# First loads in one queue, the third scaling behind the first maxima, the fourth weight a step later, and the memory term's transposes ahead of the products with V

## The chip, the cores and the metric

The kernel runs on one core of a Trainium2 chip. The time is in microseconds of the device, for one execution. The engines are TensorE (PE: matrix products and transposes; PEld: its weight loads), VectorE (DVE), ScalarE (ACT), GpSimd (POOL) and SyncE (SP), which here issues DMAs; ScalarE issues a few as well.

## What is computed

A block of three parts, over 4 x 8 heads, 576 positions and 64 values for each head:

```python
scores = scale * np.matmul(q, k.transpose(0, 1, 3, 2))
scores = np.where(causal, -1000000000.0, scores)
a = np.exp(scores - scores.max(-1, keepdims=True))
a /= a.sum(-1, keepdims=True) + 1e-09
local = np.matmul(a, v)
q_p = phi(q)                       # where(q > 0, q, exp(q) - 1) + 1
mem_out = (q_p @ M_prev) / (q_p . z_prev + 1e-06)
x = g * mem_out + (1 - g) * local  # g = sigmoid(beta), one for each head
x = ((x @ w1) * (x @ w2) @ w3) @ w_out
h = x @ w_in
out = (h - np.tanh(h)) @ w_out2
```

The weights come as 64-bit floats; the kernel decodes each tile of 128 x 512 of them into two 32-bit parts.

## The kernel before

The program has three stages. The first is attention (about 0 to 240 us), the second the two products `x @ w1` and `x @ w2` with the product that follows, the third `h` and the output. `w3` and `w_out` are multiplied with each other ahead of time, during attention ("folds"), which is why weights are decoded there.

Attention goes over 16 pairs of heads, each in four steps of query rows (`GROUPS`): blocks 0 and 1 of 128 rows, block 2, block 3, and the last 64 rows. A step `m` is numbered through, 64 in all, and the loop of lines 771 to 820 does two at once. In order of the text, one round does: `recip` and `norm` of the steps m-2 and m-1 (the reciprocal sums on VectorE, then the normalisation of the weights p on GpSimd); `scores` and `rmax` of m and m+1 (products into PSUM, maxima on VectorE); `work(m)`, which is the exponentials of step m on ScalarE and one round of the background list; the products with V, `av`, of the pair before; `flush_t`, the four transposes of one tile of the memory term (`mt<-ident,mw` in the rows), where one is due; some fold products (`pieces`, `fo` in the rows); the transposes `trans` of the normalised weights (`t<-ident,p`), each copied out of PSUM by ScalarE or VectorE; then `work(m + 1)`, more pieces and the transposes of the step after. Each engine runs its instructions in the order of this text (`Ordered`), so an instruction that waits holds up all behind it on its engine. `psT`, which takes the transposes of both kinds, has two PSUM tiles, and the scores have two as well (`SB`).

The background list (`background`, `decode`) decodes one weight tile at a time in several moves, one for each step: a clamp (`T<-raw`) and a scaling (`E<-raw`) on GpSimd, a scaling and a conversion on ScalarE, a joining on VectorE, which frees the raw buffer (there are three) for the next load, a rounding to the high part on GpSimd (`wa<-T`, `zs<-T` and the like) and the low part on VectorE. `m >= coming[0]` and `LEAD` set when the next tile begins: one step after the last for the first `LEAD` tiles, two steps after it from then on. Up to step `SHORT` = 9 the list comes behind the exponentials of a step, afterwards ahead of them.

The start: pair 0's q and k come in three pieces of 128, 192 and 256 columns (`qk_cols`, lines 334, 336 and 339), the first two in SP's queue, the third in ACT's, where the gates' `beta` stands behind it. VectorE scales q piece by piece (`first_q`, lines 350 to 352). `scores(0)` needs the first two pieces, `scores(1)` the third. `fill` puts products of a constant tile, which nothing reads, into TensorE's order: seven at the start, six ahead of step 2's scores and three ahead of its transposes.

Of the kernel before, what the change touches and what calls it, by code (L numbers as in the profile page):

```python
# [33 lines left out]
def block_kernel(ctx, tc, qk, qt, vt, mp, zp_d, beta, w1, w2, w3t, wo, wi, wo2, ident_d, mask_d, out):  # L34
# [26 lines left out]
    PE, DV, AC, PO, SP = [Ordered(e) for e in (nc.tensor, nc.vector, nc.scalar, nc.gpsimd, nc.sync)]  # L61
# [62 lines left out]
    class Decoder:  # L124
# [14 lines left out]
        def step(self):  # L139
            while self.loaded and len(self.active) < self.width:  # L140
                raw, dst = self.loaded.popleft()
                self.reading += 1
                self.active.append(dec_ops(raw, dst, self.lo_on, self.whole, self.hip, self.x))
            if not self.active:
                return False
            gen = self.active.popleft()
            r = next(gen, 2)
            if r == 1:
                self.reading -= 1
                self.load()  # L150
            if r == 2:
                self.done += 1
            else:
                self.active.append(gen)
            return True
# [14 lines left out]
    def mm(o, lhsT, rhs, start, stop):  # L170
        return PE.matmul(o, lhsT, rhs, start=start, stop=stop).ins
# [8 lines left out]
    ZB, FLAG, WAIT = 3, 1, 2  # L180
    PIECES = (1, 2, 0, 2)
    MEM, ROOM = 12, (1.5, 1.5, 1.75)
    LEAD, SHORT, TB, WX = 3, 9, 4, (0, 1, 2, 3, 4, 5)
    MS, FS, FS5 = 4, 3, 6
    FILL = {None: 7, "s": {2: 6}, "t": {2: 3}}
    PO_ = "xzw"
# [17 lines left out]
    def qk_cols(P, c, queue=SP):  # L204
        if P not in qk_t:
            qk_t[P] = apr.tile([128, 2, 576], F32, tag="r", name="r")
        queue.dma_start(out=qk_t[P][:, :, c], in_=qk[P].rearrange("p (a n) -> p a n", a=2)[:, :, c])

    def load_v(P):
        SP.dma_start(out=V[P % 2], in_=vt[P].rearrange("p (t h d) -> p t h d", t=5, h=2))  # L210
# [121 lines left out]
    if True:  # L332
# [3 lines left out]
        qk_cols(0, slice(128, 320))  # L336
        mraw = stg["T"].tile([128, 512], F32, tag="T", name="mraw")
        AC.dma_start(out=mraw[:, 0:128], in_=mask_d)
        qk_cols(0, slice(320, 576), AC)
        AC.dma_start(out=gates, in_=beta.partition_broadcast(128))  # L340
        warm = mraw[:, 128:512].bitcast(BF16)
        DV.memset(warm, 0)
# [3 lines left out]
        def first_q(a, e, P=0):  # L346
            q = qk_t[P][:, 0, a:e]
            DV.tensor_scalar(out=q, in0=q, scalar1=0.125, scalar2=None, op0=ALU.mult)

        first_q(0, 128)  # L350
        first_q(128, 320)
        first_q(320, 576)
        AC.activation(out=identb, in_=ident, func=AF.Copy)
        AC.activation(out=maskb, in_=mraw[:, 0:128], func=AF.Copy)
        AC.activation(out=gates, in_=gates, func=AF.Exp, scale=-1.0)
# [44 lines left out]
        def scores(m):  # L400
            P, us = step(m)
            q, k = qk_t[P][:, 0], qk_t[P][:, 1]
            hr = [(h, slice(64 * h, 64 * h + 64)) for h in range(2)]
            sc = sc_t[m] = pss.tile([128, 2, 512], F32, tag="sc", name="sc")
            qs = [(h, r, y, slice(64 * y, 64 * y + 64)) for y in range(2) for h, r in hr]
            for u, a in us:
                if u == 4:
                    continue
                K = 128 * (u + 1)
                for h, r, y, c in qs:  # L410
                    mm(sc[c, h, a:a + K], q[r, 128 * u + 64 * y:128 * u + 64 * y + 64], k[r, 0:K], True, False)
                for h, r, y, c in qs:
                    mm(sc[c, h, a + 128 * u + 64 * y:a + 128 * u + 128], identb[r, r], maskb[r, 0:128 - 64 * y], False, True)
            if us[0][0] == 4:
                for x in range(2):
                    for h, r in hr:
                        y = x ^ h
                        mm(sc[r, y, 0:288], q[r, 512:576], k[r, 288 * y:288 * y + 288], True, y == 0)
                for h, r in hr:
                    mm(sc[r, 1, 224:288], identb[r, r], maskb[r, 0:64], False, True)  # L420
# [185 lines left out]
        def mem_b(tl, qp):  # L606
            t = ps["t"]()
            for hp in range(4):
                tp(t[:, hp * 128:hp * 128 + 128], qp[:, hp * 128:hp * 128 + 128])
            for i in range(2):  # L610
                copy(mem_t["q"][i][:, :, tl * 128:tl * 128 + 128],
                     t[:, 256 * i:256 * i + 256].rearrange("p (a b) -> p a b", a=2),
                     on_act=i == 0 or not in_order[0])
# [72 lines left out]
        def flush(k, ok):  # L686
            if not (late and late[0][0] <= fstep[0] and late[0][1] == k and ok):
                return False
            _, _, x, y = late[0]
            return k == "t" or finished[0] >= 8 * ((x * N + N - 1) // 576) + 8  # L690

        def flush_t():
            if flush("t", True):
                _, _, x, y = late.popleft()
                mem_b(x, y)
                held[0] -= 1
# [14 lines left out]
        def background(m):  # L711
            used = [0, 0, 0]

            def advance(j):
                nonlocal used
                used = [u + n for u, n in zip(used, j[0])]
                j[0] = next(j[1], None)
                if j[0] is None:
                    jobs.remove(j)
                    active[0] -= j[2]  # L720

            for j in [*jobs]:
                if j[1] is not mem_job:
                    advance(j)
            if m >= coming[0] and begun[0] < len(fold_seq) and active[0] < TB:
                k = fold_seq[begun[0]]
                if k[0] not in range(8) or len(coming) - 1 - folded[0] < ZB + 2:
                    if k[0] in range(8):
                        coming.append(k)
                    begun[0] += 1  # L730
                    g = decode(raws[live[0]])
                    live[0] += 1
                    jobs.append([next(g), g, 1])
                    used[2] += 0.7
                    active[0] += 1
                    coming[0] = m + (1 if m < LEAD else 2)
            for j in [*jobs]:
                if j[1] is mem_job and not any(n and u + n > c for u, n, c in zip(used, j[0], ROOM)):
                    advance(j)
# [8 lines left out]
        def fill(n):  # L748
            for _ in range(n):
                mm(spare, warm[:, 0:128], warm[:, 128:640], True, True)  # L750
# [10 lines left out]
        def work(h):  # L761
            fstep[0] = h
            if h >= SHORT:
                background(h)
            if h < NM:
                exps(h)
            if h < SHORT:
                background(h)

        m = 0  # L770
        while m < NM + 3 or jobs or late or folded[0] < 16 or begun[0] < len(fold_seq):
            P, s = divmod(m, 4)
            fstep[0] = m
            if 2 <= m <= NM:
                for h in (m - 2, m - 1):
                    recip(h)
                for h in (m - 2, m - 1):
                    norm(h)
            if m < NM:
                fill(FILL["s"].get(m, 0))  # L780
                for h in (m, m + 1):
                    scores(h)
                    rmax(h)
                if m == 0:
                    set_gates()
                if m == 2:
                    first_q(0, 576, 1)
            work(m)
            if 1 <= P <= 16:
                av(P - 1, s // 2)  # L790
                if s == 2 and P + 1 < 16:
                    load_v(P + 1)
            trs = 0 <= m - WAIT < NM
            flush_t()
            pieces(m, PIECES[s])
            if trs:
                fill(FILL["t"].get(m, 0))
                for u in GROUPS[(m - WAIT) % 4]:
                    trans((m - WAIT) // 4, u)
            work(m + 1)  # L800
            sums = flush("o", True)
            if not (sums and not fold_open[0]):
                pieces(m + 1, PIECES[s + 1])
            if trs:
                for u in GROUPS[(m + 1 - WAIT) % 4]:
                    trans((m + 1 - WAIT) // 4, u)
            if sums and not fold_open[0]:
                flush_o()
            if s == 0 and 1 <= P <= 16 - RB:
                load_qk(P + RB - 1)  # L810
            if s == 0 and 1 <= P < 15:
                scale_q(P + 1)
            if not todo and not raws and not wdec[0]:
                wdec[0] = Decoder(w_items[NE:], 2, 3)
                wdec[0].done, wdec[0].total = NE, 16
            if m == NM - 2:
                gate.update({e.engine: tail[e.engine] for e in (AC, DV)})
            if m == NM:
                gate[PO.engine] = tail[PO.engine]
            m += 2  # L820
# [369 lines left out]
```

## Time and profile before

| | us |
|---|---|
| median of 3 runs | 968.78 (968.11 to 969.84) |
| the profiled execution | 971.45 |
| its span, first to last instruction | 969.7 |
| TensorE busy | 943.9 |
| VectorE, ScalarE, GpSimd busy | 675.8, 623.1, 408.1 |

A busy time is the sum of the engine's instructions. A row of the timeline gives the start, the time and, in brackets, how long the engine had been idle before it and whose work or transfer ended last. The granted clock is the share of TensorE's full clock in a stretch.

### The profile page before, as it was taken

To read this page: it belongs to the slowest core of one execution; us is meant where nothing else is said; L and a number is where in the kernel's file an instruction comes from. 1 tells how busy PE (TensorE), PEld (TensorE's weight loads), DVE (VectorE), ACT (ScalarE), POOL (GpSimd) and SP (SyncE) were. 2 spreads that over 40 slices of the span, in tenths; PEclk is the share of its full clock that TensorE was granted. 3 is DMA by queue.
4 is the path that set the end of the run, shared out by engine and by line. 5 is a ranking of instruction groups with operands and counts; after the bars stand their busy time and mean duration, and the time that the engine had idled before them with its cause. 6 is when DMAs were issued, how large, how long until landed. Compare 5 with 4: busy or idle time off the path is not lost.

```text
span 969.7 us, 16290 instructions
## 1 busy us (share of the span) xinstructions
PE 943.9 (97%) x5928; PEld 816.4 (84%) x5928; DVE 675.8 (70%) x1185; ACT 623.1 (64%) x1398; POOL 408.1 (42%) x500
## 2 busy tenths in 40 slices
PE   6899999999999999999999999999999999999998
PEld 3466666567989999999999999999999989999996
DVE  5778868897776743534424588887787887878875
ACT  5688887786546551323625587687777766776864
POOL 3768867786474521202406862222222222222222
PEclk9899999999999999999999999999999999999999
DMA  6455435422344530101401100000000000000000
GB/s 216 155 169 168 158 127 183 135 75 85 128 149 146 183 114 31 55 22 44 153 22 45 44 1 1 1 33 1 1 33 1 33 1 1 33 1 1 33 1 33
DMA packets 26080, 68.29 MB, mean 70 GB/s; under 512 B 4880, under 2 KB 5904, under 8 KB 26000
## 3 DMA queue, kind: packets, MB, share of 16 engines
q1 hardware_dynamic: 25296, 66.86, 20.8%
q8 instruction: 46, 0.75, 0.3%
q10 hardware_dynamic: 704, 0.40, 0.2%
q14 instruction: 34, 0.28, 0.1%
HBM read 62.53 MB, written 4.72 MB: 69 GB/s over the span
## 4 chain that ended last, share of the span: by engine, by line
PE 84%; DVE 7%; ACT 4%; POOL 2%; issue 1%; DMA 1%; ACTq 0%; DVEq 0%; POOLq 0%; SPq 0%
PE o L50 24%; PE h L50 21%; PE ab L50 19%; PE x L50 10%; PE sc L50 3%; PE t L50 3%; PE fo L50 3%; DVE st L50 2%; ACT p L50 2%; PE mo L50 2%; POOL p L50 1%; DMA r<-in_qk 1%; DVE g L50 1%; DVE mst L50 1%; DVE T L50 1%
## 5 line engine op out<-in xcount | busy, mean ns | idle before, releaser
L50 POOL TENSOR_TENSOR gl<-s,gh 128x384 fp32r<-128x384 f32 x96 | 99.7, 1038 | 288.0 <-ACT gh L50 274.9
L50 PE MATMUL x<-abh,wf 128*128 128x384 f32 x384 | 107.0, 342 | 1.1 <-ACT abh L50 1.1
L50 ACT ACTIVATE s<-u,pc 128x384 f32<-128x384 f32 x192 | 107.7, 613 | 0.6 <-POOL gl L50 0.6
L50 PE MATMUL ab<-xh,wa 128*128 128x384 f32 x384 | 106.9, 338 | 0.7 <-ACT xh L50 0.6
L50 POOL TENSOR_SCALAR p<-p,st 128x128 f32<-128x128 f32 (+2 forms) x144 | 86.1, 616 | 47.2 <-DVE st L50 41.0
L50 PE MATMUL ab<-xh,wb 128*128 128x384 f32 x384 | 105.9, 336 | 0.0
L50 DVE SCALAR_TENSOR_TENSOR s<-s,u 128x384 f32<-128x384 f32 x96 | 83.9, 874 | 26.8 <-ACT s L50 25.9
L50 ACT ACTIVATE p<-sc,st 128x128 f32<-128x128 f32 (+2 forms) x144 | 78.3, 556 | 29.7 <-DVE st L50 25.8
L50 ACT ACTIVATE u<-u,pc 128x384 f32<-128x384 f32 x96 | 59.4, 619 | 46.8 <-DVE s L50 46.8
L50 DVE TENSOR_TENSOR a<-ab,a 128x384 f32<-128x384 f32 x48 | 26.4, 552 | 77.4 <-PE ab L50 77.4
L50 PEld LDWEIGHTS x<-abh,wf 128*128 128x128 f32 x384 | 70.2, 188 | 5.6 <-issue 3.9
L50 POOL TENSOR_SCALAR E<-raw 128x512 f32<-128x512 f32 x72 | 53.9, 749 | 48.5 <-DVE z2p L50 13.1
L50 DVE TENSOR_TENSOR t<-h,t 128x384 f32<-128x384 f32 x96 | 53.1, 553 | 28.0 <-ACT t L50 27.5
L50 PEld LDWEIGHTS ab<-xh,wa 128*128 128x128 f32 x384 | 70.1, 188 | 2.0 <-ACT xh L50 0.9
L50 ACT ACTIVATE u<-h 128x384 f32<-128x384 f32 x96 | 46.7, 487 | 38.9 <-PE h L50 38.8
L50 PEld LDWEIGHTS ab<-xh,wb 128*128 128x128 f32 x384 | 70.1, 188 | 0.3 <-issue 0.3
L50 POOL TENSOR_SCALAR T<-raw 128x512 f32<-128x512 f32 x72 | 53.7, 746 | 39.2 <-DMA raw<-in_wo 12.0
L50 PE MATMUL sc<-r 64*64 64x128 f32 (+4 forms) x640 | 64.5, 457 | 5.8 <-DMA r<-in_qk 2.9
L50 DVE SCALAR_TENSOR_TENSOR s<-s,s 128x384 f32<-128x384 f32 x96 | 63.9, 665 | 8.7 <-DVE s L50 0.5
L50 PE MATMUL t<-ident,p 128*128 128x128 f32 (+1 forms) x400 | 58.2, 279 | 11.9 <-POOL p L50 4.4
L50 PEld LDWEIGHTS t<-ident,p 128*128 128x128 f32 (+1 forms) x400 | 45.2, 140 | 24.4 <-POOL p L50 6.4
L50 ACT ACTIVATE E<-raw 128x512 uint16<-128x512 uint32 x72 | 57.2, 795 | 12.6 <-POOL E L50 12.3
(208 smaller groups left out, 2538.3 us busy)
## 6 DMA issues: line engine op xcount, KB each, us to landing
raw<-in_wo SPq DMA_DIRECT2D x24, 512.0 KB, 3.5
r<-in_qk SPq DMA_DIRECT2D x15, 576.0 KB, 5.9
raw<-in_w3t SPq DMA_DIRECT2D x16, 512.0 KB, 4.0
raw<-in_w SPq DMA_DIRECT2D x16, 512.0 KB, 3.7
raw<-in_wi SPq DMA_DIRECT2D x16, 512.0 KB, 3.5
v<-in_vt SPq DMA_DIRECT2D x16, 320.0 KB, 2.9
mw<-in_qt SPq DMA_DIRECT2D x18, 256.0 KB, 3.5
out<-ob SPq DMA_DIRECT2D x18, 256.0 KB, 2.2
```

Of the source, the lines that this page charges most:

```text
L50: i = call(*args, **kw)
```

## The change

Four places. The third piece of pair 0 is loaded by SP's queue, behind the first two. Its scaling on VectorE stands behind the maxima of step 0. `LEAD` is 2 in place of 3, so that the fourth weight tile begins at step 4 in place of 3, and all after it later by one step (the last eight by two: the last at step 58, before at 56). `flush_t` stands ahead of `av`.

```diff
-    LEAD, SHORT, TB, WX = 3, 9, 4, (0, 1, 2, 3, 4, 5)
+    LEAD, SHORT, TB, WX = 2, 9, 4, (0, 1, 2, 3, 4, 5)
...
-        qk_cols(0, slice(320, 576), AC)
+        qk_cols(0, slice(320, 576))
         AC.dma_start(out=gates, in_=beta.partition_broadcast(128))
...
         first_q(0, 128)
         first_q(128, 320)
-        first_q(320, 576)
...
                 for h in (m, m + 1):
+                    if h == 1:
+                        first_q(320, 576)
                     scores(h)
                     rmax(h)
...
             work(m)
+            flush_t()
             if 1 <= P <= 16:
                 av(P - 1, s // 2)
                 if s == 2 and P + 1 < 16:
                     load_v(P + 1)
             trs = 0 <= m - WAIT < NM
-            flush_t()
             pieces(m, PIECES[s])
```

VectorE's first instructions (`r` holds q and k, `st` the maxima), before and then now:

```order
L50 TENSOR_SCALAR r<-r 128x128
L50 TENSOR_SCALAR r<-r 128x192
L50 TENSOR_SCALAR r<-r 128x256
L50 TENSOR_REDUCE st<-sc 128x2 x3
L50 TENSOR_SCALAR gates<-gates 128x16
```

```order
L50 TENSOR_SCALAR r<-r 128x128
L50 TENSOR_SCALAR r<-r 128x192
L50 TENSOR_REDUCE st<-sc 128x2 x2
L50 TENSOR_SCALAR r<-r 128x256
L50 TENSOR_REDUCE st<-sc 128x2
L50 TENSOR_SCALAR gates<-gates 128x16
```

The scaling of 256 columns has gone behind the two maxima of step 0 and stands ahead of the one of step 1.

GpSimd from the normalisation of steps 0 and 1 (`p` of 128 to 384 columns) to that of steps 2 and 3 (512 and 576 columns) and the next, before and then now:

```order
L50 TENSOR_SCALAR wa_275<-T 128x512
L50 TENSOR_SCALAR E<-raw 128x512
L50 TENSOR_SCALAR T<-raw 128x512
L50 TENSOR_SCALAR p<-p,st 128x512 x2
L50 TENSOR_SCALAR p<-p,st 128x576
L50 TENSOR_SCALAR wb_343<-T 128x512
L50 TENSOR_SCALAR E<-raw 128x512
L50 TENSOR_SCALAR wa_375<-T 128x512
L50 TENSOR_SCALAR T<-raw 128x512
L50 TENSOR_SCALAR p<-p,st 128x128 x2
```

```order
L50 TENSOR_SCALAR wa_275<-T 128x512
L50 TENSOR_SCALAR E<-raw 128x512
L50 TENSOR_SCALAR p<-p,st 128x512 x2
L50 TENSOR_SCALAR p<-p,st 128x576
L50 TENSOR_SCALAR wb_341<-T 128x512
L50 TENSOR_SCALAR T<-raw 128x512
L50 TENSOR_SCALAR wa_372<-T 128x512
L50 TENSOR_SCALAR E<-raw 128x512
L50 TENSOR_SCALAR p<-p,st 128x128 x2
```

The fourth weight's `T<-raw` has gone behind the normalisation; ahead of the one after it stand a rounding and an `E<-raw`, where a `T<-raw` stood.

TensorE around the third tile of the memory term (`o` is the product with V, `fo` a fold), before and then now:

```order
L50 MATMUL o<-g_2177,v_107 64x256 x2
L50 MATMUL o<-g_2177,v_107 64x128 x2
L50 MATMUL mt<-ident,mw 128x128 x4
L50 MATMUL fo<-fo_980,zs 128x512 x3
L50 MATMUL t<-ident,p 128x128 x8
L50 MATMUL fo<-fo_1177,zs 128x512 x3
L50 MATMUL fo<-fo_1374,zs 128x512 x3
L50 MATMUL t<-ident,p 128x128 x4
```

```order
L50 MATMUL mt<-ident,mw 128x128 x4
L50 MATMUL o<-g_2164,v_107 64x256 x2
L50 MATMUL o<-g_2164,v_107 64x128 x2
L50 MATMUL fo<-fo_1396,zs 128x512 x3
L50 MATMUL t<-ident,p 128x128 x12
```

The memory term's four transposes have gone ahead of the products with V, and two of the three groups of folds have left this round.

## Rows read from the trace of the kernel before

**Rows 1.** The page: busy time of each engine, over the whole span.

```profile
PE 943.9 (97%) x5928; PEld 816.4 (84%) x5928; DVE 675.8 (70%) x1185; ACT 623.1 (64%) x1398; POOL 408.1 (42%) x500
```

**Rows 2.** Windows: stretch, us, busy of the five engines, granted clock, DMA share, GB/s.

```profile
20.00:30.00 10.00, 6.11 (x63) 3.57 (x67) 7.29 (x17) 8.72 (x24) 6.74 (x10) 0.87 0.64 219
30.00:40.00 10.00, 9.66 (x94) 5.19 (x88) 7.06 (x17) 4.97 (x13) 6.28 (x12) 0.79 0.31 96
```

**Rows 3.** Timeline of TensorE from 6 to 31 us.

```profile
6.67 1.13 PE L50 MATMUL sc<-r 64*64 64x256 f32 x8 [1.40 <-DVE r L50]
...
10.76 1.87 PE L50 MATMUL sc<-r 64*64 64x384 f32 x8 [2.86 <-DMA r<-in_qk]
...
12.62 1.96 PE L50 MATMUL spare<-mraw 128*128 128x512 bf16 x6
14.51 1.09 PE L50 MATMUL sc<-r 64*64 64x512 f32 x8
...
25.40 0.33 PE L50 MATMUL t<-ident,p 128*128 128x128 f32 x1 [2.67 <-POOL p L50]
...
27.93 1.30 PE L50 MATMUL t<-ident,p 128*128 128x128 f32 x5 [0.88 <-DVE g L50]
29.16 1.99 PE L50 MATMUL sc<-r 64*64 64x512 f32 x8
```

**Rows 4.** Timeline of the other engines and SP's queue, 0 to 16 us.

```profile
0.73 1.32 SPq L50 DMA_DIRECT2D r<-in_qk  x2
...
10.74 0.29 DVE L50 TENSOR_SCALAR r<-r 128x256 f32<-128x256 f32 x1 [4.12 <-DMA r<-in_qk]
...
10.95 1.02 DVE L50 TENSOR_REDUCE st<-sc 128x2 f32<-128x256 f32 x2
...
11.62 0.64 POOL L50 TENSOR_SCALAR T<-raw 128x512 f32<-128x512 f32 x1
12.05 0.22 ACT L50 ACTIVATE gates<-gates 128x16 f32<-128x16 f32 x1 [7.15 <-DMA gates<-in_beta]
...
15.22 2.75 POOL L50 TENSOR_SCALAR p<-p,st 128x128 f32<-128x128 f32 x6 [2.97 <-DVE st L50]
```

**Rows 5.** DMA issues of 0 to 40 us: size, median us to landing.

```profile
r<-in_qk ACTq DMA_DIRECT2D x1, 256.0 KB, 9.1
r<-in_qk SPq DMA_DIRECT2D x1, 192.0 KB, 4.9
...
gates<-in_beta ACTq DMA_DIRECT2D x1, 8.0 KB, 9.7
```

**Rows 6.** Timeline of SP, GpSimd and ScalarE, 19 to 27 us.

```profile
19.10 0.33 SPq L50 DMA_DIRECT2D raw<-in_wo  x1
...
20.87 0.68 POOL L50 TENSOR_SCALAR E<-raw 128x512 f32<-128x512 f32 x1
...
23.07 0.64 POOL L50 TENSOR_SCALAR T<-raw 128x512 f32<-128x512 f32 x1 [1.52 <-DMA raw<-in_wo]
...
23.80 2.94 POOL L50 TENSOR_SCALAR p<-p,st 128x512 f32<-128x512 f32 x3
...
26.65 0.60 ACT L50 ACTIVATE g<-t 128x512 f32<-128x512 f32 x1 [0.94 <-PE t L50]
```

**Rows 7.** Timeline of TensorE: transposes after each memory tile, and one fold group.

```profile
89.56 0.63 PE L50 MATMUL t<-ident,p 128*128 128x128 f32 x4 [0.62 <-ACT g L50]
...
90.72 0.85 PE L50 MATMUL fo<-wb,zs 128*128 128x512 f32 x3
...
123.83 0.66 PE L50 MATMUL t<-ident,p 128*128 128x128 f32 x4 [1.04 <-DVE mq L50]
...
166.31 0.66 PE L50 MATMUL t<-ident,p 128*128 128x128 f32 x4 [1.27 <-ACT g L50]
```

**Rows 8.** Waits, whole span: us in total, times, longest.

```profile
POOL p L50 <- DVE st L50: 41.0, 23, 3.4
...
PE t L50 <- POOL p L50: 4.4, 5, 2.7
```

## The prediction

> **What bounds the kernel now.** I read the page's busy line first, then the windows and the granted clock, then TensorE's own order of time, then the engines that its early waits name. TensorE is busy for 943.9 of 969.7 us [rows 1], so only 25.8 us of idle time and whatever runs at the lower clock can be won; work moved on another engine counts only where TensorE waits for it. The waits lie at the start. TensorE stands 2.86 us before the third block of scores, 2.67 us before the transposes of step 4 and 0.88 us soon after [rows 3]. Behind these gaps the granted clock falls: its mean is 0.87 from 20 to 30 us and 0.79 from 30 to 40 us [rows 2], and one level is 2.4 GHz, the other 1.2. Eight score products of 512 columns take 1.99 us there, against 1.09 us earlier [rows 3]. So the start has three losses: a late load, a normalisation that comes late, and the clock that this idle time cost. Every microsecond that TensorE gains early stays gained if it then runs without new waits, because the rest of the program is nearly all TensorE.
>
> **Part A: the first loads and the third scaling.** The third piece of pair 0 (256 KB, on ACT's queue) lands 9.1 us after its issue, the second piece (192 KB, on SP's) after 4.9 us, and the 8 KB of gates, behind the third piece on ACT's queue, after 9.7 us [rows 5]. VectorE's scaling of the third piece begins at 10.74 us, ends at 11.03, and only then come the two maxima of step 0 (1.02 us), because they stand behind it on VectorE [rows 4]. ScalarE's gates Exp stands ahead of the first exponentials and runs at 12.05 us [rows 4]. The change removes both waits. On SP the third piece is issued at about 0.73 + 1.32 = 2.05 us [rows 4]; with the 4.9 us that the second one needed it lands by 7.0 us, ahead of the weights that now follow it. The gates leave one issue earlier and have no 256 KB in front of them in their queue.
>
> What binds then is order: the scores of step 0 end at about 6.67 + 1.13 + 0.1 = 7.9 us [rows 3], the two maxima take 1.02 us, the third scaling 0.29 us, so TensorE has all it needs for step 1 at 9.2 us instead of 11.03: a gain of 1.8 us even if the second piece lands no sooner. The upper bound is GpSimd. Its second weight operation ends at 11.62 + 0.64 = 12.3 us, and the first normalisation stands behind it, at 15.22 us now [rows 4]: 2.9 us at most. The six filling products (1.96 us) stay and hide ScalarE's exponentials of step 0 [rows 3]; without that cover TensorE would wait for them all the same. I take the middle, **-2.4 us**; both ends are kept, and zero if the gates still land at 12 us.
>
> SP pays one more issue ahead of the three weights: two issues take 1.32 us, 0.66 each [rows 4]. I leave that in the bounds, since the bytes in front of the weights are the same. The Trainium skill ("DMA: Bandwidth & Descriptors", section Rules for kernel authors) speaks against this part: spreading transfers over issuing engines brings no bandwidth, it saves issue time alone, so that going back to one queue would give up that time and win no bytes. By it A would be 2.4 - 0.66 = 1.7 us and the total 963.1 us, instead of what the rows give below; the 9.1 us for the third piece, against 4.9 for the second, shows that order among the bytes counts here, which the rule does not speak of.
>
> **Part B: the fourth weight a step later.** GpSimd's first clamp of the fourth weight stands ahead of the normalisation of steps 2 and 3. SP issues that load at 19.10 us, the clamp waits 1.52 us for it, runs at 23.07 us for 0.64, and the normalisation starts at 23.80, though GpSimd's previous operation had ended at 20.87 + 0.68 = 21.55 us [rows 6]. Removed from there: 2.25 us of TensorE's 2.67 us wait. Behind the normalisation the load, about 4 us, has 2 to 3 us more of cover, so I cost the moved clamp at nothing; if the cover falls short, the next operation in line is the rounding of another weight, which TensorE needs only steps later. Next late is ScalarE: its copy of the transposes runs at 26.65 us, after 0.94 us of idle [rows 6]; so at least 0.94 us moves with it. Between 0.94 and 2.25 I take **-1.6 us**.
>
> **Part C: the clock.** Lost clock is (1 - 0.87) x 10 + (1 - 0.79) x 10 = 3.4 us [rows 2]. It fell after TensorE had stood 2.67 us and, within 3 us more, 0.88 us again [rows 3]. With B the long stop shrinks to about 0.4 us, so I expect the upper level to hold. Not all comes back: at full speed TensorE reaches the next steps before ScalarE, VectorE and GpSimd, which had used the slow stretch to catch up. Bounds 0 and -3.4; half of it, **-1.8 us**, is what I take.
>
> **Part D: the memory term's transposes.** Only three of them run in this loop. After each, the fourth or later transposes of weights wait, because the pool of two PSUM tiles is one short until the memory tile is copied out: 0.62, 1.04 and 1.27 us, 2.93 together [rows 7]. With the products with V between, that copying goes on beside 20 or 8 products. Nothing is added. Bounds 0 and -2.93; the copying may still be late behind the 8 products, so I take less than half, **-1.2 us**.
>
> **Part E: what slips.** From the fourth weight on every item begins one step later, the last eight two (the last at step 58, not 56). A group of three fold products takes 0.85 us [rows 7]; by the order of the two programs the loops at steps 10 and 44 each have two groups fewer to fill TensorE with, and the last loop two more. The same work is done later, at no cost while TensorE is busy, but where other engines are late it no longer fills a gap. On SP the loads of weights change places with those of q, k and V; both are issued loops ahead of their use, so I cost that at nothing, and if it were late it would show as rival 5's wait does. Bounds 0 and two groups, 1.7 us: **+0.6 us**.
>
> **Sum.** -2.4 - 1.6 - 1.8 - 1.2 + 0.6 = -6.4 us. Against the profiled execution (span 969.7, 971.45 us with what lies around it) that is 965.05 us. The median of the three runs, 968.78, is 2.67 us below that execution, and the same work would be done there: **962.4 us**. About 0.2% (1.9 us) is what a measurement of this kernel tells from no change.
>
> **The rivals.** (1) *The clock still falls*: waits of 0.4 us and 0.9 us remain near each other, and C is nothing; -4.6 us, 964.2. For it: TensorE stands early as often as before; against it: the longest stop goes. 0.16. (2) *The start does not move*: the gates or the first two weights land when they did, and ScalarE still begins at 12.05 us; A is nothing; -4.0 us, 964.8. For it: the gates' 8 KB took 9.7 us and their size is not why; against it: what stood before them in their queue is gone. 0.10. (3) *More than forecast*: all bounds of A to D are met and nothing slips; -2.9 - 2.25 - 3.4 - 2.93 = -11.5 us, 957.3. For it: each wait has its cause in the list; against it: other engines are close behind. 0.08. (4) *The gain is given back*: ScalarE and GpSimd bind until the folds begin, so TensorE waits again for what it gained; under 1.9 us left, about 968. 0.08. (5) *Slower*: the step's parity turns for all later weights. GpSimd used to run the clamp, which waits for no engine, right ahead of each normalisation; now the rounding, which waits for VectorE, and the second scaling stand there. If they end after the reciprocals are ready, the normalisation is late and TensorE waits for it in each of 27 loops (steps 4 to 58). TensorE waited five times for normalised weights, 4.4 us in all, the longest 2.7, so the others average (4.4 - 2.7) / 4 = 0.43 us [rows 8]; 27 x 0.43 = 11.6, with the sum +5.2 us, 974.0. It decides from the point where GpSimd no longer waits for the reciprocals: it waits 41.0 us for them now, 23 times, 1.8 us each [rows 8], and that reserve speaks against it. 0.07.
>
> **How the numbers follow.** The forecast has 0.51 (its own range 960 to 964.5). Faster by over 0.2% (under 966.8): 0.51 + 0.16 + 0.10 + 0.08 = 0.85. Same: 0.08. Slower: 0.07. The range takes in rivals 1 to 3 with their bounds, and leaves out the slower case and most of the one that gives back: 957.3 to 967 us.
>
> **What the profile would show.** A: scores of step 1 at 9 us or sooner, the first exponentials by 9.5 us, the first normalisation at 12.3 to 13.4 us. B: no wait of GpSimd for a load around 18 to 24 us, and a normalisation of step 2 at 18 to 19.5 us. C: a granted clock of 1.00 in each stretch after 20 us, and 512-column scores at 1.09 us there. D: under 0.5 us of waiting behind each of the three memory transposes. E: no wait over 1 us at steps 10 and 44. I would be wrong if the gates Exp still stood at 12 us, if the clock fell elsewhere, or if TensorE's waits for normalised weights grew beyond 4.4 us between 50 and 230 us.

## The result, and the profile after

The changed kernel takes 960.06 us (median of 4 runs, 959.9 to 960.65) against 969.31 us before in the same session (4 runs, 968.11 to 969.89): a ratio of 0.9907, 95% interval 0.989 to 0.9924, so 9.25 us less. Forecast were 962.4 us, from 957.3 to 967. The profiled execution after took 960.0 us, with a span of 958.2. The two spans differ by 11.5 us, more than the medians, because the execution that was profiled before was 2.1 us above its median.

The page's busy line after, to be laid beside [rows 1]:

```profile
PE 942.0 (98%) x5927; PEld 815.6 (85%) x5928; DVE 677.5 (71%) x1185; ACT 621.8 (65%) x1398; POOL 407.0 (42%) x500
```

The engines do the same work. TensorE's idle time fell from 25.8 to 958.2 - 942.0 = 16.2 us. The windows of the same stretches as [rows 2], and two more (the columns are those of [rows 2]):

```profile
0.00:10.00 10.00, 8.08 (x44) 2.73 (x45) 2.16 (x7) 3.93 (x13) 1.04 (x9) 1.00 0.73 229
20.00:30.00 10.00, 8.19 (x58) 4.43 (x59) 8.33 (x14) 7.94 (x23) 8.23 (x13) 0.83 0.38 150
30.00:40.00 10.00, 8.44 (x93) 4.94 (x93) 8.46 (x20) 8.22 (x26) 7.25 (x12) 1.00 0.51 176
40.00:60.00 20.00, 19.66 (x200) 12.55 (x197) 14.58 (x33) 17.34 (x49) 14.45 (x23) 1.00 0.65 215
```

From 30 to 40 us the clock holds, but from 20 to 30 us it still falls, to a mean of 0.83. Lost there: (1 - 0.83) x 10 = 1.7 us of full clock, against 3.4 before. TensorE's timeline, the counterpart of [rows 3]:

```profile
6.86 2.42 PE L50 MATMUL sc<-r 64*64 64x384 f32 x6
...
9.08 0.77 PE L50 MATMUL sc<-r 64*64 64x384 f32 x2
...
11.21 1.09 PE L50 MATMUL sc<-r 64*64 64x512 f32 x8
...
19.52 0.33 PE L50 MATMUL t<-ident,p 128*128 128x128 f32 x1
20.19 0.98 PE L50 MATMUL t<-ident,p 128*128 128x128 f32 x7 [0.34 <-POOL p L50]
22.79 0.84 PE L50 MATMUL t<-ident,p 128*128 128x128 f32 x5 [1.62 <-ACT g L50]
23.57 1.98 PE L50 MATMUL sc<-r 64*64 64x512 f32 x8
```

Step 1's scores no longer wait for a load. The stop of 2.67 us before the first transpose of step 2 (the prediction calls them those of step 4, the step at which the loop runs them) is gone; the 0.34 us before the next seven stood there before as well. The second stop, behind them, has grown from 0.88 to 1.62 us. The scores of step 6 start at 23.57 us instead of 29.16, still at the lower clock (1.98 us for what takes 1.09 at the upper). The other engines in the same stretch (compare [rows 4, 6]):

```profile
5.70 0.21 ACT L50 ACTIVATE gates<-gates 128x16 f32<-128x16 f32 x1 [1.06 <-DMA gates<-in_beta]
...
7.10 1.02 DVE L50 TENSOR_REDUCE st<-sc 128x2 f32<-128x256 f32 x2 [1.33 <-PE sc L50]
8.04 0.28 DVE L50 TENSOR_SCALAR r<-r 128x256 f32<-128x256 f32 x1
8.23 0.37 ACT L50 ACTIVATE p<-sc,st 128x128 f32<-128x128 f32 x1 [2.31 <-DVE st L50]
9.36 0.64 POOL L50 TENSOR_SCALAR T<-raw 128x512 f32<-128x512 f32 x1 [8.43 <-DMA raw<-in_wo]
...
12.47 2.95 POOL L50 TENSOR_SCALAR p<-p,st 128x128 f32<-128x128 f32 x6 [0.99 <-DVE st L50]
...
18.77 2.59 POOL L50 TENSOR_SCALAR p<-p,st 128x512 f32<-128x512 f32 x3
...
22.69 1.15 POOL L50 TENSOR_SCALAR T<-raw 128x512 f32<-128x512 f32 x1
```

The first normalisation moved from 15.22 to 12.47 us, that of steps 2 and 3 from 23.80 to 18.77, with no wait for a load in front of it. The fourth weight's clamp follows at 22.69 us. The loads, beside [rows 5]:

```profile
r<-in_qk SPq DMA_DIRECT2D x1, 256.0 KB, 4.7
r<-in_qk SPq DMA_DIRECT2D x1, 192.0 KB, 4.0
...
gates<-in_beta ACTq DMA_DIRECT2D x1, 8.0 KB, 4.0
```

The third piece lands 4.7 us after its issue instead of 9.1, the gates 4.0 us instead of 9.7. TensorE's waits from 60 us to the end of the attention stage, all of them, with the three memory tiles (`mt`) that [rows 7] belong to:

```profile
84.11 0.66 PE L50 MATMUL mt<-ident,mw 128*128 128x128 f32 x4
87.23 0.66 PE L50 MATMUL t<-ident,p 128*128 128x128 f32 x4 [0.31 <-DVE mq L50]
117.28 0.66 PE L50 MATMUL mt<-ident,mw 128*128 128x128 f32 x4
...
151.56 0.66 PE L50 MATMUL mt<-ident,mw 128*128 128x128 f32 x4
154.67 1.11 PE L50 MATMUL t<-ident,p 128*128 128x128 f32 x8 [0.33 <-DVE mq L50]
156.11 0.30 PE L50 MATMUL t<-ident,p 128*64 128x128 f32 x1 [0.33 <-DVE g L50]
163.03 0.85 PE L50 MATMUL t<-ident,p 128*128 128x128 f32 x6 [0.76 <-ACT g L50]
167.63 0.98 PE L50 MATMUL t<-ident,p 128*128 128x128 f32 x7 [0.34 <-POOL p L50]
```

The stretch of 60 to 220 us as one window, before and then after:

```profile
60.00:220.00 160.00, 154.31 (x1459) 101.27 (x1459) 133.36 (x277) 130.32 (x351) 123.48 (x176) 1.00 0.43 145
```

```profile
60.00:220.00 160.00, 157.62 (x1472) 104.03 (x1472) 137.38 (x289) 131.18 (x358) 123.53 (x179) 1.00 0.44 144
```

TensorE stood 5.7 us in it before and stands 2.4 us now. That is 3.3 us of the gain, far from the start, where the forecast had put a gain of 1.2 us for part D and a loss of 0.6 us for part E. `e12_flush_back` below divides it: 1.8 us go with the memory term's transposes, 1.5 us with the weights' new steps.

### The profile page after: what moved, and what is told of

It reads as the page before. It is cut to its first block, busy times and chain, and to the rows that moved or that the text cites. A ratio compares the mean times of both kernels' runs of the same rounds, so it can differ in the third digit from the quotient of the medians.

```text
span 958.2 us, 16304 instructions
## 1 busy us (share of the span) xinstructions
PE 942.0 (98%) x5927; PEld 815.6 (85%) x5928; DVE 677.5 (71%) x1185; ACT 621.8 (65%) x1398; POOL 407.0 (42%) x500
## 4 chain that ended last, share of the span: by engine, by line
PE 90%; DVE 6%; ACT 2%; issue 1%; DMA 1%; POOL 1%; SPq 0%; DVEq 0%; ACTq 0%; POOLq 0%
PE o L50 25%; PE h L50 21%; PE ab L50 20%; PE x L50 11%; PE sc L50 4%; PE t L50 4%; PE fo L50 4%; DVE st L50 2%; PE mo L50 2%; ACT p L50 1%; DVE g L50 1%; DVE T L50 1%; DVE mst L50 0%; POOL p L50 0%; DMA r<-in_qk 0%
## 5 line engine op out<-in xcount | busy, mean ns | idle before, releaser
L50 POOL TENSOR_SCALAR p<-p,st 128x128 f32<-128x128 f32 (+2 forms) x144 | 86.0, 616 | 36.4 <-DVE st L50 26.8
L50 POOL TENSOR_SCALAR T<-raw 128x512 f32<-128x512 f32 x72 | 56.6, 787 | 39.1 <-DMA raw<-in_wo 11.5
L50 POOL TENSOR_SCALAR E<-raw 128x512 f32<-128x512 f32 x72 | 51.1, 710 | 47.2 <-DVE z2p L50 12.8
L50 DVE COPY_PREDICATED s<-u,t 128x384 f32<-128x384 uint32 x96 | 58.7, 612 | 8.9 <-DVE s L50 0.5
L50 PE MATMUL x<-abl,wf 128*128 128x384 f32 x192 | 64.9, 338 | 0.0
L50 ACT ACTIVATE E<-raw 128x512 uint16<-128x512 uint32 x72 | 57.3, 796 | 11.5 <-POOL E L50 11.2
```

The source lines that it names most:

```text
L50: i = call(*args, **kw)
```

## The experiments

Theory 1 was that each of the edits takes its own wait, and that the parts add up. Its rivals were that an earlier start is eaten by the wait for the fourth weight, that the new order of the later weights costs what it gives, and that the start alone moves everything. All ratios below are against the kernel before on the same chip in the same session (medians of 969.5 to 970.0 us, 17 to 29 runs), so that a difference of about 1.5 us between two experiments is not clear of noise. The gains in us are worked out from the ratios, unless medians are named; the differences of the medians are up to about 1 us off them.

**One part alone.** The loads with the scaling (`e1_loads`):

```diff
-        qk_cols(0, slice(320, 576), AC)
+        qk_cols(0, slice(320, 576))
...
-        first_q(320, 576)
...
+                    if h == 1:
+                        first_q(320, 576)
```

> The kernel before with the third piece in SP's queue and its scaling behind the first maxima; the fourth weight and the memory term's transposes stay where they were. If the parts add up (theory 1): 2.5 to 3.5 us faster than before, as the first normalisation came 2.75 us and the scores of step 2 3.3 us earlier in the changed kernel; the clamp of the fourth weight still waits about 1.5 us for its load and the granted clock still falls for some 7 us. If the earlier start is eaten by the wait for the fourth weight (theory 2, the parts need each other): under 1 us faster. If the start alone moves everything (theory 3): 8 us or more faster, and the later waits gone as well.

Measured: 968.02 us, ratio 0.9985 (0.9975 to 0.9996): 1.5 us faster, between 0.4 and 2.4. The start of the changed kernel is all there, but the clamp of the fourth weight, ahead of the normalisation of steps 2 and 3 as before, waits again, though 0.58 us and not the 1.5 us expected (GpSimd's timeline, then the window of TensorE's clock):

```profile
11.45 2.94 POOL L50 TENSOR_SCALAR p<-p,st 128x128 f32<-128x128 f32 x6 [1.50 <-DVE st L50]
...
18.27 0.63 POOL L50 TENSOR_SCALAR T<-raw 128x512 f32<-128x512 f32 x1 [0.58 <-DMA raw<-in_wo]
19.00 3.03 POOL L50 TENSOR_SCALAR p<-p,st 128x512 f32<-128x512 f32 x3
```

```profile
20.00:30.00 10.00, 7.84 (x45) 4.22 (x46) 6.38 (x13) 6.88 (x18) 7.28 (x12) 0.66 0.47 166
```

The clock lost from 20 to 30 us is (1 - 0.66) x 10 = 3.4 us, all of the loss of before, only earlier. So the loads take their own wait and nothing more. The third theory falls, and theory 1 is met at less than its number; the second, under 1 us, lies inside this interval and falls only with the next run.

The load alone, VectorE's order as before (`e4_queue`):

```diff
-        qk_cols(0, slice(320, 576), AC)
+        qk_cols(0, slice(320, 576))
```

> The kernel before with the third piece in SP's queue alone; VectorE still scales it ahead of the first maxima. The third piece landed by 6.7 us in the changed kernel, before the maxima could begin (7.1 us). If the queue is all that counts: 2.5 to 3.5 us faster, as the kernel with both edits. If the place of the scaling counts too: at least 1 us less than that one.

Measured: 967.34 us, ratio 0.9971 (0.9959 to 0.9982), 2.8 us faster, between 1.7 and 4.0. The place of the scaling brings nothing that can be seen: without it the gain is, if anything, larger. The scaling ran at 6.99 us and the two maxima with the third in one go from 7.20 us, where they started at 6.58 us in the run before this one; the piece lands about when the maxima can begin.

The weights' steps alone (`e2_lead`):

```diff
-    LEAD, SHORT, TB, WX = 3, 9, 4, (0, 1, 2, 3, 4, 5)
+    LEAD, SHORT, TB, WX = 2, 9, 4, (0, 1, 2, 3, 4, 5)
```

> The kernel before with the fourth weight (and all later ones) a step later, nothing else. Theory 1: the normalisation of steps 2 and 3 starts about 2.2 us earlier, the loss of clock shrinks from 3.4 to under 2 us, and the other waits between 60 and 240 us shrink by some 2 us: 4 to 6 us faster. Rival (the later order of the folds and of GpSimd costs as much as it gives): within 2 us of before, with GpSimd's normalised weights waited for more often.

Measured: 963.63 us, ratio 0.9933 (0.9917 to 0.9949), 6.5 us faster. This one number is two thirds of the whole change. The rival falls: TensorE waited for normalised weights 0.3 us in all, against 4.4 us [rows 8]. The longest stop among the transposes, 2.1 us, is now for ScalarE's copy, and in this trace the clock held all the same (1.00 from 20 to 40 us):

```profile
PE t L50 <- ACT g L50: 4.3, 4, 2.1
PE sc L50 <- DMA r<-in_qk: 3.1, 1, 3.1
...
PE t L50 <- POOL p L50: 0.3, 1, 0.3
```

The memory transposes alone (`e3_flush`):

```diff
             work(m)
+            flush_t()
...
-            flush_t()
             pieces(m, PIECES[s])
```

> The kernel before with the memory term's transposes ahead of the products with V, nothing else. Theory 1: the waits of 0.62, 1.04 and 1.27 us behind the three memory transposes fall below 0.5 us each: 1.5 to 2.5 us faster. Rival (the copying waits for ScalarE and VectorE and not for the place on TensorE, so that the wait moves to the next transposes): within 0.7 us of before.

Measured: 968.98 us, ratio 0.9993 (0.998 to 1.0006): not to be told from nothing. Two of the three waits did fall, from 0.62 to none and from 1.04 to 0.48 us, the third only from 1.27 to 1.10. The single parts add up to 1.5 + 6.5 + 0.7 = 8.7 us (7.9 by the medians), the whole is 9.25: within the noise there is no need of an effect of the parts on each other.

**What about the weights' steps it is.** First the whole change without it (`e5_no_lead`):

```diff
-    LEAD, SHORT, TB, WX = 2, 9, 4, (0, 1, 2, 3, 4, 5)
+    LEAD, SHORT, TB, WX = 3, 9, 4, (0, 1, 2, 3, 4, 5)
```

> The changed kernel with the fourth weight and all later ones back at their old steps (loads, scaling and memory transposes stay changed). If the parts add up, the loads' 1.5 us and the transposes' 0.5 us are what is left: 1.5 to 2.5 us faster than before. If the step of the weights only works together with the loads (they need each other): 4 us or more faster even without it, since the sum of the single parts, 1.5 + 5.9 + 0.5 = 7.9 us, would then leave something over for the pair.

Measured: 967.01 us, ratio 0.9976 (0.9962 to 0.999), 2.3 us faster than before, as the sum of its parts. `LEAD` does two things: it puts the fourth weight behind the normalisation of steps 2 and 3, and it turns the parity of all later weights. Two runs part them. The fourth weight at step 4, the rest at their old steps (`e9_parity`, from the changed kernel):

```diff
-                    coming[0] = m + (1 if m < LEAD else 2)
+                    coming[0] = m + (1 if m < LEAD or m == 4 else 2)
```

> The changed kernel, with the fourth weight at step 4, but the fifth at step 5 and all later ones at their old steps. If the step of the weights gains by what it does at step 4 (the normalisation no longer behind the clamp, less clock lost): as the changed kernel, 8 to 9.5 us faster than before. If it gains by the later order (folds one and three to a round instead of two and two, scaling and rounding ahead of the normalisation): 3 us or more of the gain is gone, and the waits between 60 and 240 us are those of the kernel before, some 6 us.

The fourth at step 3, the rest at the new steps (`e10_later`, from the kernel before):

```diff
-                    coming[0] = m + (1 if m < LEAD else 2)
+                    coming[0] = m + (1 if m < LEAD else 3 if m == LEAD else 2)
```

> The kernel before, with the fourth weight still at step 3, but the fifth at step 6 and all later ones at the steps of the changed kernel; loads and transposes as before. The reverse of the run before this one in the list: if the place at step 4 is what counts, within 1.5 us of before; if the later order counts, 3 us or more faster, with the clock still lost after 20 us.

Measured: `e9_parity` 966.0 us, ratio 0.9965 (0.995 to 0.9979), 3.4 us faster than before; `e10_later` 966.45 us, ratio 0.9961 (0.9946 to 0.9976), 3.8 us faster. So with the fourth weight's place kept and the later order taken back, (0.9965 - 0.9907) x 969.7 = 5.6 us of the change's gain are gone; the later order alone gives 3.8 us to the kernel before; and the fourth weight's place gives 3.4 - 2.3 = 1.1 us (`e9_parity` beside `e5_no_lead`, whose intervals overlap) or 6.5 - 3.8 = 2.7 us (`e2_lead` beside `e10_later`). By these numbers the later order is the larger half, though the noise does not decide between 3.8 and 2.7 us. Where it works, TensorE's windows show: `e9_parity` first, from 30 and from 100 us, then the changed kernel from 100 us.

```profile
30.00:40.00 10.00, 6.58 (x77) 3.99 (x79) 7.53 (x20) 7.42 (x23) 7.24 (x13) 1.00 0.62 204
...
100.00:140.00 40.00, 39.27 (x355) 25.76 (x347) 30.70 (x67) 33.29 (x91) 29.77 (x45) 1.00 0.45 149
140.00:180.00 40.00, 37.95 (x367) 24.18 (x367) 35.62 (x77) 31.02 (x85) 29.69 (x43) 1.00 0.46 154
180.00:220.00 40.00, 38.69 (x365) 25.61 (x363) 35.65 (x76) 31.30 (x86) 30.87 (x41) 1.00 0.37 125
```

```profile
100.00:140.00 40.00, 40.00 (x380) 26.86 (x379) 32.48 (x70) 33.85 (x93) 31.39 (x47) 1.00 0.52 166
140.00:180.00 40.00, 38.23 (x371) 24.54 (x372) 32.32 (x74) 31.30 (x84) 27.44 (x43) 1.00 0.40 130
180.00:220.00 40.00, 39.78 (x356) 26.35 (x350) 38.51 (x76) 31.57 (x88) 31.98 (x44) 1.00 0.35 123
```

From 30 to 40 us TensorE stands 3.4 us instead of 1.6, longest for GpSimd's rounding (1.68 us) and ScalarE's exponentials (1.23 us). That the fifth weight, right behind the fourth, is the reason was not tested; `e8_before_fill` below, with the old order throughout, stands 3.3 us there as well. From 100 to 220 us it stands 4.1 us instead of 2.0. Over 60 to 220 us the later order is worth 5.7 - 4.2 = 1.5 us in the trace of `e10_later` beside the kernel before, and 4.3 - 2.4 = 1.9 us in that of the changed kernel beside `e5_no_lead`. Which property of the new order it is, the other place of the clamp and the rounding on GpSimd, the rounds with three groups of folds and one instead of two and two, or the other place of the low parts on VectorE, was not parted; no run here changed one of these alone.

**The clock.** Twelve filling products in the stop before the transposes of step 2, in the kernel before (`e8_before_fill`):

```diff
-    FILL = {None: 7, "s": {2: 6}, "t": {2: 3}}
+    FILL = {None: 7, "s": {2: 6}, "t": {2: 3, 4: 12}}
```

> The kernel before with twelve filling products ahead of the transposes of step 2, where TensorE stands 2.67 us. If the clock that is lost after 25 us was lost to that stop: the granted clock holds from 20 to 40 us (before: 0.87 and 0.79, 3.4 us of full clock) and the kernel is 1.5 to 3.4 us faster than before, without any of the four edits. If the clock falls for another reason, or the other engines need the slow stretch: within 1 us of before.

Measured: 967.21 us, ratio 0.9973 (0.996 to 0.9987), 2.6 us faster. In its timeline the products fill the stop, and the scores of step 6 run at the upper clock:

```profile
19.96 2.76 PE L50 MATMUL spare<-mraw 128*128 128x512 bf16 x12
24.29 0.74 PE L50 MATMUL t<-ident,p 128*128 128x128 f32 x5 [0.34 <-POOL wb L50]
24.96 1.09 PE L50 MATMUL sc<-r 64*64 64x512 f32 x8
```

Nothing that is computed is changed and the transposes wait for the same normalisation, so this is the price of the clock that the stop cost: 2.6 us (1.3 to 3.9) of the 3.4 that the windows had put down to it. In that figure is what the second stop gave, which shrank from 0.88 to 0.34 us. The trace as a whole can't be laid beside that of before: its third piece landed 5.8 us after the issue instead of 9.1, with the loads in the same order, and step 2's scores start at 11.81 us instead of 14.51. Of the 5.2 us between the two spans, 2.7 us are there before the filling products begin. Then the same in the changed kernel, where the stop behind it has grown to 1.62 us (`e6_after_fill`):

```diff
+    FILL = {None: 7, "s": {2: 6}, "t": {2: 3}, "u": {4: 7}}
...
             if trs:
+                fill(FILL["u"].get(m, 0))
                 for u in GROUPS[(m + 1 - WAIT) % 4]:
```

> The changed kernel with seven filling products (512 columns, nothing reads them) ahead of the transposes of step 3, where TensorE stands 1.62 us. If the clock falls at 22 us because TensorE stood there: the granted clock holds 1.00 from 20 to 30 us, the scores of 512 columns take 1.09 us, 1 to 2 us faster than the changed kernel. If the clock falls for an earlier reason or the products delay the transposes: no gain, or up to 1.5 us slower than it.

Measured: 958.88 us (958.83 to 960.59), ratio 0.9897 (0.9875 to 0.9918). Its clock holds, and the same eight products come at 22.35 us:

```profile
20.00:30.00 10.00, 8.38 (x71) 4.56 (x69) 8.95 (x14) 8.23 (x22) 7.75 (x13) 1.00 0.50 157
```

By the medians it is 1.2 us faster than the changed kernel, by the intervals it can't be told from it. In the traces that lead is there ahead of the filling products: step 2's scores start at 10.05 us instead of 11.21, and the spans differ by the same 1.2 us. What the clock gave back went into the next stop, 1.52 us for ScalarE's copy at 29.17 us instead of 0.34 at 30.73.

**Single parts taken back from the changed kernel.** The scaling ahead of the first maxima again (`e11_scale_back`), and the same with the seven filling products (`e13_fill_scale_back`):

```diff
         first_q(128, 320)
+        first_q(320, 576)
...
-                    if h == 1:
-                        first_q(320, 576)
```

> The changed kernel with the third piece scaled ahead of the first maxima again. The two kernels with the load alone changed were 2.8 us faster without this edit and 1.5 us with it, with intervals that overlap. If the place of the scaling is worth the 1 us that the two maxima take: 0.5 to 1.3 us slower than the changed kernel. If the load is all that counts, since the piece lands before the maxima can begin: within 0.7 us of the changed kernel (about 9 us faster than before).

> The kernel with the seven filling products (1.2 us faster than the changed kernel by the medians) with the third piece scaled ahead of the first maxima again: the best of the tried parts together, if the place of the scaling costs. If it does: 957.5 to 958.5 us. If the place is worth its 1 us: 959 to 960 us.

Measured: 959.72 us, ratio 0.9891 (0.9872 to 0.991), and 959.46 us, ratio 0.9891 (0.9872 to 0.991). The first is 0.3 us below the changed kernel, the second 0.6 us above `e6_after_fill`. That is inside the range which I had expected if the place is worth 1 us; but the two differ in sign and both are inside the noise, so that no worth of the place can be told. In the profiled execution of `e11_scale_back` the clock held from 20 to 30 us without any filling products:

```profile
20.00:30.00 10.00, 6.96 (x60) 4.12 (x60) 9.19 (x16) 8.30 (x24) 8.63 (x13) 1.00 0.49 181
```

```profile
22.61 0.74 PE L50 MATMUL t<-ident,p 128*128 128x128 f32 x5 [1.55 <-ACT g L50]
```

So a stop of 1.6 us costs clock in some executions and not in others. The two traces also show what the clock was worth here: step 2's scores start at 11.23 us in this one and at 11.21 in the changed kernel, which then loses 1.7 us of clock and ends only 0.3 us later (spans of 957.9 and 958.2 us).

The memory transposes behind the products with V again (`e12_flush_back`):

```diff
             work(m)
-            flush_t()
...
             trs = 0 <= m - WAIT < NM
+            flush_t()
```

> The changed kernel with the memory term's transposes behind the products with V again. With the weights' new steps alone the waits behind the three memory transposes were 0.89, 0.62 and 0.89 us, in the changed kernel 0.31, 0 and 0.33: 1.5 to 2 us slower than the changed kernel. If the wait is only put off to the next transposes, as the kernel with this edit alone (0.7 us, not clear of nothing) may say: within 0.7 us of the changed kernel.

Measured: 960.88 us, ratio 0.9908 (0.9891 to 0.9924), 1.2 us above `e11_scale_back` of the same session and 0.8 us above the changed kernel's own median: less than expected, and not clear of noise. The trace shows the waits as expected:

```profile
87.71 0.66 PE L50 MATMUL t<-ident,p 128*128 128x128 f32 x4 [0.89 <-DVE mq L50]
...
121.62 0.63 PE L50 MATMUL t<-ident,p 128*128 128x128 f32 x4 [0.62 <-ACT g L50]
...
156.18 1.09 PE L50 MATMUL t<-ident,p 128*128 128x128 f32 x8 [0.89 <-DVE mq L50]
```

0.89 + 0.62 + 0.89 = 2.4 us, against 0.31 + 0.33 = 0.64 in the changed kernel. The window of 60 to 220 us says the same:

```profile
60.00:220.00 160.00, 155.83 (x1462) 102.81 (x1461) 135.93 (x284) 131.25 (x357) 123.67 (x180) 1.00 0.43 144
```

TensorE stands 4.2 us here, 2.4 us in the changed kernel and 5.7 us in the kernel before: 1.8 us go with the transposes' place, and 1.5 us are left for the weights' steps. The two profiled executions, with starts alike, differ by the same 1.8 us of span (960.0 and 958.2).

## Why the prediction was right, and where it was not

The sign and the range held; the forecast of 6.4 us was 2.9 us short of 9.25. That 960.06 us still lies inside owes something to luck: the range reaches down to 957.3 us because of rival 3, all bounds of A to D met and nothing slipping, and what made the gain larger was E, which had the wrong sign. By its own steps:

- **Part A, 2.4 us forecast.** Its times came as said: the third piece landed by 2.05 + 4.7 = 6.8 us (forecast 7.0), the rest of step 1's scores started at 9.08 us (9.2), the first normalisation at 12.47 us (12.3 to 13.4). The worth was 1.5 us with the scaling moved and 2.8 us with the load alone. The rows it was read from were a late draw: the 9.1 us of the third piece are the longest in the five traces that leave it in ACT's queue (5.8 to 9.1 us), against 4.3 to 5.3 us in the nine that move it. The bound on GpSimd did not bind: its second clamp was over by then, and the normalisation waited 0.99 us for the reciprocals. No worth of the moved scaling can be told. What the Trainium skill's rule ("DMA: Bandwidth & Descriptors", section Rules for kernel authors) would have cost, 0.66 us for the issue that SP takes over, can't be told at the weights: the first clamp ran at 7.2 to 10.0 us in the five traces, at 7.8 to 9.4 us in the nine. What counted is what stands ahead of a transfer: the gates, of the same size and in the same queue, landed 6.9 to 9.7 us after their issue behind the third piece and 3.7 to 4.6 us without it.
- **Part B, 1.6 us.** The normalisation of steps 2 and 3 came at 18.77 us (forecast 18 to 19.5), and it was ScalarE's copy that was late next, as the lower bound had it. Measured: 1.1 to 2.7 us with the clock that goes with it.
- **Part C, 1.8 us.** The size came out in the windows, the reason did not, so that this is luck. I expected the clock to hold from 20 us on; it fell, for half as long, and the windows give 3.4 - 1.7 = 1.7 us. That lost clock need not all come back as time was right: the 1.7 us that the changed kernel still lost cost it 0.3 us of span beside `e11_scale_back`. The stop that I had set at 0.4 us was followed by one of 1.62 us before the next transposes, which the working of part B should have shown: ScalarE's copy could move by as little as 0.94 us where TensorE moved by 2.25, and the difference of 1.3 us is a wait for that copy.
- **Part D, 1.2 us.** In the traces 1.8 us (2.4 - 0.64), by waits and by window; by the times 0.7 us alone and about 1 us taken back, neither clear of noise.
- **Part E, +0.6 us: the step that failed.** It priced the later weights by the two groups of folds that leave a round, and called the rest of the turned parity a risk (rival 5) with no gain on the other side. The later order gives 3.8 us alone (2.3 to 5.2) and 5.6 us in the changed kernel, by the ratios; the traces place 1.5 to 1.9 us of it between 60 and 220 us, and of the 5.6 us another 1.9 from 30 to 40 us. With E at -3.8 instead of +0.6 the sum is -10.8, within 1.6 us of what was measured. Rival 5 fell: GpSimd still has reserve ahead of the normalisation, and TensorE waits for normalised weights 1.0 us in all instead of 4.4. GpSimd's row after, beside [rows 8]:

```profile
POOL p L50 <- DVE st L50: 26.8, 21, 4.0
...
PE t L50 <- POOL p L50: 1.0, 3, 0.3
```

A third of GpSimd's reserve is used up (26.8 us instead of 41.0), which is what rival 5 was afraid of, and yet TensorE's waits for the normalised weights became fewer. Rivals 1, 2 and 4 fell with the total, and rival 2 with the gates at 5.70 us; rival 1's premise, that the clock still falls, was half right. Rival 3 came nearest in time, but not by what it said: the clock still fell, and the waits of part D were not all gone.

## What to carry to other kernels

When a change shifts a repeated piece of background work by a step, count the rounds it passes through before pricing it: here 1 to 3 us at the place the edit was made for came with about 4 to 5 us, by the ratios, from the 27 rounds behind it, and the waits of before, round by round (0.1 to 1.3 us each), would have given the room for a gain as well as for a loss. Put a transfer that the first work needs ahead of bulk loads in the same queue, and look at what stands ahead of the small ones too. Where a stop also costs clock, products that nothing reads can buy that part back: 2.6 us behind the stop of 2.67 us. But lost clock is not yet lost time: an execution that kept its clock at the later stop of 1.6 us stood 1.46 us for ScalarE's copy at the next transposes (30.05 us in `e11_scale_back`), where the one that lost it stood 0.34.

## What was not expected of the hardware

The kernel before spreads from 967.0 to 973.2 us over the 72 runs of the three sessions, the changed one only from 959.9 to 960.65 us in its four. In part the mean granted clock of the span goes with it: of the 26 runs before of the first session, those with 0.992 took 969.9 to 972.5 us, those with 0.997 took 967.1 to 970.8; in the third, runs with 0.996 took 968.2 to 973.0. Loss of clock at the start is thus not a fixed price: beside a stop of 1.62 us the changed kernel's trace lost 1.7 us of clock, beside one of 1.55 us that of `e11_scale_back` lost none, and the order on TensorE is the same in both.

Two more things at the start differ from execution to execution. One is the landing of the third piece, which spreads by 3.3 us in ACT's queue and by 1.0 us in SP's. The other is TensorE's level in the first 10 us: step 0's eight products of 256 columns took 0.66 us in five of the traces and 1.13 us in the other nine, among them those of the kernels before and after. The column of the granted clock does not show it: it reads 1.00 from 0 to 10 us in all but one of the fourteen. So two traces are laid side by side from a place at which they are known to be alike.
